# A state-space layer joined with linear attention: kernel products for two channels at a time, their halves summed in the next step

## The chip, the cores and the metric

The program runs on one core of one Trainium2 chip. A core has a matrix engine (TensorE, "PE" in the profile; "PEld" is its loading of weights, which runs beside it), three engines that work on vectors (VectorE "DVE", ScalarE "ACT", GpSimd "POOL"), a sync engine ("SP") that issues most of the transfers, and 16 DMA engines that carry them out. Tiles lie in an on-chip memory of 128 partitions; results of TensorE land in a separate small memory, PSUM, and another engine has to copy them out ("evict" them) before TensorE can use them again. Each engine works through its own list of instructions strictly in order, and waits at an instruction until what it needs is there.

The metric is the device time of one execution, in microseconds (us).

## The reference, cut to what matters

The input `A_u` has 2048 time steps of 512 channels. Two layers read it, and a gate mixes them.

```python
# layer A: a state-space model, as a long convolution
logdA = dt * (A_re + 1j * A_im)                    # 512 channels x 128 states
P = exp(logdA[:, :, None] * l[None, None, :])      # l = 0..2047
K = einsum("dn,dnl,dn->dl", Cc, P, dt * Bc).real   # one filter of 2048 taps per channel
y = irfft(rfft(u padded) * rfft(K padded))[:2048] + u * Dskip
# layer B: attention without a softmax over time, 32 heads of 16
phi = concat(softmax(+p), softmax(-p)); o = (phi_q @ kv) / (phi_q @ z + 1e-6); b = o @ wo
g = sigmoid((x * gate_w).sum(-1)); out = g * a + (1 - g) * b
```

What the change touches is `K`: a sum over 128 states for each of 512 channels and 2048 lags.

## The kernel before, in words

**Stages.** The first part (to about 100 us of the trace) loads the inputs, builds sine and exponential tables, transposes the input, computes the keys of layer B and the spectrum of the input. The second part, the convolution stage, goes through the 512 channels in 16 units of 32 channels, together with the queries of layer B.

**One unit.** A lag is split into a coarse and a fine part: lag = 64 x (0..31) + (0..63), so that the filter is a product of two small tables, summed over the 128 states. VectorE builds the coarse table `A` in two multiplications (`half`, called by A1 and A2, line 1053), which differ in which product of the complex factors they take; these are the "halves". It builds the fine table `R` in two more (lines 1071 and 1075, from an exponential `E` by ScalarE, its shifted twin `El` by VectorE, line 1013, and sines and cosines `cs` by ScalarE). `A` has 128 columns a channel: 2 halves x 2 parts (paired with the two parts of `R`) x 32 coarse lags. TensorE then multiplies `A` by `R` (`kgen_chunk`, lines 168 to 177, the rows "kps"): 32 weight columns at a time, four channels side by side in the array's four column strips. Here the constant `FOURS` (line 95) decides how the halves are summed:

- In 13 of the 16 units each channel takes four products, which PSUM adds up: 128 products a unit.
- In units 0, 7 and 15 VectorE adds the halves of the table first (`a3`, line 1064), and each channel takes two products: 64 products a unit.

Either way a unit leaves 512 numbers in each partition of PSUM. Two units share one PSUM tile and one eviction to `KD` (`kd`, line 1090); unit 14 is evicted alone, and unit 15 alone in two pieces.

Then comes the first half of a Fourier transform of the filters (`fft_stage_a`, lines 180 to 183, the rows "psA"): `KD` for four channels is the weights (64 columns are the fine lags), and a table `W1` of 128 columns (32 frequencies x 4 channels) is the moving operand; 16 products a unit, evicted to `XA`. Further on: second half of the transform ("psB", line 189, evicted to `XK`), multiplication with the input's spectrum ("t", line 1185), the way back ("psz", evicted to `Zr`, written to memory as `Zd`, line 1230, and read back transposed as `ZT`, line 1239), the last sum ("psy", line 1295), the gate (lines 1317 to 1323) and the output (line 1334).

**Groups.** Units 0 to 11 are taken in groups of four (128 channels), units 12 and 13 together (64 channels), unit 14 alone (32 channels), and unit 15 alone, by a path without the trip through memory (lines 1251 and 1308).

**What sets the order.** Nothing is scheduled at run time. The program is a list of nodes, each for one engine; a string (`ORDER`) is the order in which all nodes are issued, `SIDES` says for each eviction that could go to ScalarE or VectorE which of them takes it, and `RINGS` which PSUM ring a tile comes from. Each engine's list follows `ORDER`. Buffers come in rings of fixed size: one `KD`, one `A`, two `R`, one `ZT` (it shares its buffer, "ax", with layer B's rows `ax`), and so on; and there are eight lanes for transfers under way. Tables of ScalarE (sine, or exponential and logarithm) are swapped by an instruction (line 65) wherever the order goes from one kind to the other.

Of the kernel before, what the change touches and what calls it, by code (L numbers as in the profile page):

```python
# [43 lines left out]
def build_index_cols(nc, pool):  # L44
    idx_i = pool.tile([128, 1], I32, name="idx_i")
    nc.gpsimd.iota(idx_i[:], pattern=[[0, 1]], base=0, channel_multiplier=1)
    want = (("p", 0, 127), ("p31", 0, 31), ("p63", 0, 63), ("h16", 4, 7), ("h2", 4, 1), ("s5", 5, 3), ("b5", 5, 1), ("b6", 6, 1), ("h8", 0, 7), ("h4", 0, 3))
    t = pool.tile([128, len(want)], I32, name="ii")
    f = pool.tile([128, len(want)], F32, name="if")
    for k, (name, shift, mask) in enumerate(want):  # L50
        if shift:
            nc.vector.tensor_scalar(out=t[:, k:k + 1], in0=idx_i[:], scalar1=shift, scalar2=mask,
                                    op0=ALU.arith_shift_right, op1=ALU.bitwise_and)
        else:
            nc.vector.tensor_single_scalar(out=t[:, k:k + 1], in_=idx_i[:], scalar=mask, op=ALU.bitwise_and)
    return t, f, {name: f[:, k:k + 1] for k, (name, _, _) in enumerate(want)}
# [14 lines left out]
class Plan:  # L71

    DIGITS = "0123456789abcdefghijklmnopqrstuvwxyzABCDEFGHIJKLMNOPQRSTUVWXYZ-_"
    ORDER = ("0J0K0f0g0h0L0O0N0R0S2x0c0d0e0i0j0k1c1e0M1b000102030405090a0b1I1x0u0v0w0Y1d1o1z0U1f0x0y0z0V0P0W1A0607081p1B1q1J1K1Y0l0m0n"
             "0-0Z180_0X112P1g1-2y2N1Z2Q2B130r0s0t0A0B0C1_2A2O2C1y1C0o0p0q10190D0E0F2J2K2R1h1F1D0Q1G16122L2M2T2S2F142H2U2G171S2I2D2E2V"
             "2X2W152Y4v4w1N1O1r1s1t1i1j1k4u4B4C1E4J2v2w0G0H0I1H4F4K4D4N1Q0T1a2Z4E2-2_1U1V1P301W4G4x4O1M1l1m1n4L4M591X27314H1u1v1w4R4I"
             "28214P32335a1T344V4S3520224Q2324361L4T4U55374W4X4Z56254Y393a384-51574_521R58263b3d4y3c503e535h2z2a3f5d545i293g5l3h5b2b5e"
             "3J3i5c2d5f5g5t3j5j3k5k5m2e3l3m3n3K3o3p5u5n5o5v3L5w2f3M2c2g3q3v3r5p5x3w2o2h5q3x2i3y3C3z3A3B5r5y3E3D3s3t3u3N3P3F3Q3G3H3I3O"
             "2q3R3S2k3T2j3V3X3Y3U3W3Z3-2l3_5s402m412p4342442r2s4546472n484a4f2t494h2u4b4g4m4o4i704c4d4e4p727r4n7t5z7q7s4j4k4l4q4r4s5A"
             "5B5C5D5E4t5I6_5F5G5H714z734A7674777968696a6b7c5J78757d7a7i7e7D7j6c7b7f5K7g7E7h9a6d6e7F7J9c6f5L7R7S7T7k6g7l7u6h6z7v7K7x7w"  # L80
             "7A7m5M5N7n8O6i6j6k7-7_806A5O7y7z8X6B7B8P7o8Y5P7p7C6l6m6n6p6q6r6o6C7G7H7I8K7U7V7W6t5Q8M6u8L8Q7L8U5R8V8N6s5S5T5U5V8ZaD8R6D"
             "5W5X5Y7MaE916E6F927N7P7O7Q6G5-5_606H9d8S6v9e9m9n5Z8T9f61818W6I828-8_996w62836x6J6K6L6M6N6O9ba-90639j6Pb06y93946Q6R6S6465"
             "896T8h9k8a8i6U6V8485669o6W8b9s9g678c9h7X7Y7Z6XaA8daC9t6Y6Z6-9i8p8qazaB9l9D9E9Fa_9597b18j969p9q8r988kaFaM9raJ8687889u8l8s"
             "8e8f8gaGaN9vaKcw9w9y8m8n8o8t9xbb9zcyaHaIcxaLbcb2aOaSaTb3czaPb49MaQb89N8D9A9B9C9Ocob9aRaUbhcs9UaV9Vbd8u8v8w8x8y8zb58A8B8C"
             "9P9Q8E9G9H9I8F9R9S9T9Wb6cAcBcCa0a1djdk8G8H9J9K9La2bsbtbub7cDa8a9cEcF8I9XcGcHcIaWba9Y8Jbie8a3aaaXe9dsaba4bvbwbxbedl9Z9-9_"
             "bfdpaYdqdtaZbgacbjcpcJcKcLcNcOcPbkcMblbncQadaeafdmamctdybodncqbmbBbCbJbKa5a6a7dobRbpbqbrbDdrcubEbSduagahaid7d8d9bFbLbMdz"
             "bZbNbybzbAanb-dvdwdxcrbTcvdAdBbUb_bGbHbIc0eaaobObPbQajakaldCbVeeefc1dEbWbXbYapdFdDdGebecaqc2c3c4ardOdHdPasdadbdceddIegeB"
             "eCeEeFdQdJdgdhdicbeDeheHeic5c6c7eGeIejdKcccddRcRekdSdddedfeJeKc8c9cacedLdMdNeLeMeNeOcfelemencScgcTdTdUdVchePeQeoawaxayeR"
             "cUeSatauaveTepdWdXdYcVcWdZd-d_cZcXcYclcmcneUeVc-e0eWeqeresc_d0cicjcke1d1d2d3eXeYeteuevewexeyeZe5e6e7e2e3e4e-e_d4d5d6ezeA"
             "f3f4f5f0f1f2")  # L90
    SIDES = ("101001110101011000000100111001111100000011000100010000111101010000000100001100000000010000000000000000000000100000000001"
             "00010111111100000001100101000000010")
    RINGS = ("001011011111010000001010010001001010010010100100100100000110001100010101011110011011000000000000000000001110000000000001"
             "01011110001100000000010111010011100111001011001010010100111100000111110")
    FOURS = ("0111111101111110")
# [96 lines left out]
def prepare(P, nc, g, evict, psum):  # L192
# [297 lines left out]
    xt = []  # L490
# [42 lines left out]
def keys_and_spectrum(P, nc, g, psum):  # L533
# [85 lines left out]
    def shift():  # L619
        g.UD = g.wT = None  # L620
        g.shift()
# [398 lines left out]
def plan_conv(P, nc, g, psum, r):  # L1020
# [19 lines left out]
    def kgen(units, XA, new, split=False):  # L1040
        K = Bag()
        K.done, kps, nu = [], [], len(units)
        for cc, U in enumerate(units):
# [37 lines left out]
            def kp(c=c, cc=cc, four=four):  # L1081
                if cc == 0:
                    K.ps = psum([128, 2, 4, 2, 64], "kps")
# [489 lines left out]
```

## Time and profile before

| | |
|---|---|
| Median of 3 runs | 271.82 us (270.63 to 276.2) |
| The profiled execution's own time | 270.31 us |
| Its span, first to last instruction | 268.5 us |
| Mean granted clock of TensorE | 0.923 |
| Busy share: PE, DVE, ACT, POOL | 75%, 83%, 82%, 3% |
| Instructions | 10262 |

The profile is of one execution. A group of rows gives the line, the engine, the operation, what it writes and reads, the count, the busy time and the mean of one instruction in nanoseconds (ns). The mean counts an instruction from its start to its end; where instructions overlap at the edges, the distance from one start to the next is smaller, and this distance (its "pitch") is what the instruction costs an engine that has no idle time. Lines of the timeline give start, duration, engine, line, operation and count, and in brackets how long the engine had been idle before and what ended that. Reported idle time of an engine that nobody waits for costs nothing.

### The profile page before, as it was taken

Reading aid. Unit: us, or ns where it says so; the run is one execution under the profiler, and the core shown is the slowest. Engines: PE = TensorE matmul, PEld = TensorE weight load, DVE = VectorE, ACT = ScalarE, POOL = GpSimd, SP = SyncE. Lnnn points to the kernel's source line nnn. Section 1 sums busy time; section 2 is a strip of 40 time slices with the busy share of each in tenths; the row PEclk is TensorE's granted clock in tenths of the full one; section 3 lists DMA queues with packets and bytes.
Section 4 is the critical chain, followed back from the end, with each engine's and each line's share of the span. In section 5 each row is a group of like instructions: output and inputs, shape, how many; then the busy total and the mean of one; then the engine's idle time right before and its main releaser. Section 6 shows DMA issues by size and latency. Waiting matters only on the chain. (4 is left out here: it accounts for less than half of the span.)

```text
span 268.5 us, 10262 instructions
## 1 busy us (share of the span) xinstructions
PE 202.2 (75%) x4640; PEld 140.5 (52%) x4640; DVE 224.2 (83%) x300; ACT 219.1 (82%) x265; POOL 7.6 (3%) x16
## 2 busy tenths in 40 slices
PE   1358999999886679758587877876978779789810
PEld 1247666566655434435466755464747547665600
DVE  6999768698999789999999989995999889976401
ACT  6899799989899899999999989996788897644100
POOL 7300000000000000000000000000000000000000
PEclk9999999999999959999569999996897999999955
DMA  5999510000439894048055441392686899998372
GB/s 116 145 179 224 143 42 2 1 2 2 120 95 257 243 277 160 5 115 213 6 166 147 105 156 35 128 173 68 196 258 188 168 219 246 201 235 151 60 110 44
DMA packets 71468, 36.27 MB, mean 135 GB/s; under 512 B 50304, under 2 KB 66304, under 8 KB 71424
## 3 DMA queue, kind: packets, MB, share of 16 engines
q1 hardware_dynamic: 67680, 34.83, 56.0%
q10 hardware_dynamic: 3744, 0.79, 1.6%
q8 instruction: 36, 0.59, 0.9%
q14 instruction: 8, 0.07, 0.1%
HBM read 21.12 MB, written 13.11 MB: 127 GB/s over the span
## 5 line engine op out<-in xcount | busy, mean ns | idle before, releaser
L1053 DVE TENSOR_TENSOR A<-Ctab,Dtab 128x2048 bf16<-128x2048 bf16 x32 | 38.3, 1221 | 0.2
L68 ACT ACTIVATE cs<-args 128x1024 bf16<-128x1024 f32 x32 | 30.9, 1037 | 1.9 <-issue 1.1
L65 ACT ACT_TABLE_LOAD x18 | 23.1, 1283 | 0.3
L176 PE MATMUL kps<-R,A 128*32 128x64 bf16 x1856 | 20.3, 202 | 3.3 <-issue 2.1
L176 PEld LDWEIGHTS <-A 128*32 128x32 bf16 x1856 | 18.3, 116 | 6.6 <-issue 5.3
L1071 DVE TENSOR_TENSOR R<-E,cs 128x2048 bf16<-128x2048 bf16 x16 | 19.5, 1220 | 0.6 <-ACT E L68 0.6
L140 ACT CAST XK<-psB 128x1024 bf16<-128x1024 f32 (+1 forms) x15 | 14.3, 980 | 6.5 <-PE psB L189 6.3
L1075 DVE TENSOR_TENSOR R<-El,cs 128x2048 bf16<-128x2048 bf16 x16 | 19.5, 1220 | 0.1
L1185 DVE TENSOR_TENSOR t<-XUX,XK 128x2048 bf16<-128x2048 bf16 x14 | 17.1, 1220 | 2.1 <-ACT XK L140 1.3
L1217 PE MATMUL psz<-t,TI 128*128 128x512 bf16 x60 | 16.1, 395 | 2.8 <-ACT cs L68 2.6
L806 PE MATMUL pq<-xT,Wqp 128*128 128x512 bf16 x64 | 15.8, 393 | 2.6 <-ACT KD L140 2.2
L140 ACT CAST Zr<-psz 128x1024 bf16<-128x1024 f32 x15 | 15.3, 1032 | 2.7 <-PE psz L1217 1.2
L140 ACT CAST XA<-psA 128x1024 bf16<-128x1024 f32 (+1 forms) x15 | 13.9, 972 | 3.9 <-PE psA L183 3.8
L189 PE MATMUL psB<-XA,TB 128*128 128x128 bf16 (+2 forms) x192 | 11.2, 207 | 7.3 <-issue 3.3
L68 ACT ACTIVATE Ek<-pk 128x1024 bf16<-128x1024 f32 x16 | 15.4, 1024 | 1.4 <-PE pk L679 1.3
L68 ACT ACTIVATE E<-args 128x1024 bf16<-128x1024 f32 x16 | 16.4, 1042 | 0.2 <-PE args L1004 0.2
L68 ACT ACTIVATE Eq<-pq 128x1024 bf16<-128x1024 f32 x16 | 15.5, 1061 | 0.6 <-PE pq L806 0.6
L1320 DVE TENSOR_TENSOR xT<-psy,gT 128x1024 bf16<-128x1024 f32 (+1 forms) x5 | 5.6, 1116 | 11.8 <-PE psy L1295 11.8
L710 PE MATMUL vp<-WW,xT 128*128 128x512 bf16 x64 | 15.0, 379 | 0.0
L679 PE MATMUL pk<-WW,xT 128*128 128x512 bf16 x64 | 15.0, 379 | 0.0
L189 PEld LDWEIGHTS <-TB 128*128 128x128 bf16 x192 | 9.4, 100 | 9.7 <-issue 9.2
L497 PE MATMUL xps<-ident,UD 128*128 128x128 bf16 x64 | 7.3, 293 | 7.6 <-DMA UD<-in_A_u_dram 5.6
(203 smaller groups left out, 488.6 us busy)
## 6 DMA issues: line engine op xcount, KB each, us to landing
XUX<-XUd SPq DMA_DIRECT2D x32, 256.0 KB, 4.3
XUd<-xst SPq DMA_DIRECT2D x8, 512.0 KB, 4.4
ax<-apd SPq DMA_DIRECT2D x16, 256.0 KB, 5.2
Zd<-Zr SPq DMA_DIRECT2D x15, 256.0 KB, 3.6
ZT<-Zd SPq DMA_DIRECT2D x6, 512.0 KB, 7.2
UD<-in_A_u_dram SPq DMA_DIRECT2D x16, 128.0 KB, 4.3
XUd<-xst SPq DMA_DIRECT2D x8, 256.0 KB, 5.4
out_dram<-xT SPq DMA_DIRECT2D x4, 192.0 KB, 4.2
```

Of the source, the lines that this page charges most:

```text
L65: return self.nc.scalar.preload_act_table_set(name)
L68: return self.nc.scalar.activation(**kw)
L140: self.nc.scalar.copy(out=o, in_=i)
L176: nc.tensor.matmul(kps[32 * dj:32 * dj + 32, g4, e, :], lhsT=A[:, d // 4, 32 * ka:32 * ka + 32, d % 4], rhs=R[:, kr, d, :], start=(i == 0) ...
L189: nc.tensor.matmul(ps[:, sl, :], lhsT=fc.TB[:, 3 * (r0 + sl) + 1:3 * (r0 + sl) + 3].rearrange("p a b -> p (a b)"), rhs=XA[:, r0 + sl], sta ...
L679: nc.tensor.matmul(box.ps[:, u, :], lhsT=xT[:, 2 * s2 + u, kt, :], rhs=g.WW[:, kt, :], start=(kt == 0), stop=(kt == 3))
L806: nc.tensor.matmul(box.ps[:, m - m0, :], lhsT=g.Wqp[:, kt, 128 * m:128 * m + 128], rhs=xT[:, 4 * b:4 * b + 4, kt, :], start=(kt == 0), sto ...
L1053: nc.vector.tensor_tensor(out=c.A[:, :, 64 * k:64 * k + 64, :].rearrange("p q (x b) l -> p x b q l", b=8), in0=cf.unsqueeze(2).to_broadcas ...
L1071: nc.vector.tensor_tensor(out=c.R[:, :, :, 32:64], in0=t.E[:].unsqueeze(1).to_broadcast([128, 2, 32, 32]), in1=t.cs[:], op=ALU.mult)
L1075: nc.vector.tensor_tensor(out=c.R[:, :, :, 0:32], in0=t.L[:].unsqueeze(1).to_broadcast([128, 2, 32, 32]), in1=t.cs[:, ::-1, :, ::-1], op=A ...
L1185: nc.vector.tensor_tensor(out=box.t, in0=Ls[r0 // ns].X[:], in1=box.XK[:].unsqueeze(1).to_broadcast([128, 2, 1024]), op=ALU.mult)
L1217: nc.tensor.matmul(box.ps[:, hb, :], lhsT=fc.TI[:, k].rearrange("p t h a -> p (t h a)"), rhs=box.t[:, k, 512 * hb:512 * hb + 512], start=( ...
```

## The change

- Every unit now takes the same way: for each channel two products of 64 weight columns (32 coarse lags x 2 halves), summed in PSUM over the two parts of `R`; 64 products a unit. The halves stay apart, as neighbouring columns of `A`, and so as neighbouring rows of the result. Two channels lie side by side in the array instead of four. VectorE's additions `a3` are gone.
- A unit therefore leaves 1024 numbers in each partition of PSUM instead of 512. Each unit has a PSUM tile and an eviction to `KD` of its own.
- The first half of the Fourier transform takes two channels at a time instead of four. Its table `W2` has 64 columns (32 frequencies x 2 channels) and gives both halves of a coarse lag the same entry, so that the sum over the rows adds the halves up. It takes 32 products a unit, of 64 moving columns each, instead of 16 of 128.
- `W2` lies in the place of `W1` and is made from a small table (a sine and a cosine row more) by two VectorE instructions, once the input's spectrum has used `W1`.
- The index columns move to another tile, with one column more.
- `ORDER`, `SIDES` and `RINGS` are new throughout. Among other things some evictions change engine; unit 14's way through memory now comes ahead of that of units 12 and 13; the last outputs are all issued by ScalarE's queue.

```diff
-def kgen_chunk(nc, kps, A, R, four):
-    for e in range(2):
-        for g4 in range(4):
-            terms = [(k, k) for k in range(2)] if not four else [(0, 0), (2, 0), (1, 1), (3, 1)]
-            for i, (ka, kr) in enumerate(terms):
-                for dj in range(4):
-                    d = 8 * g4 + 4 * e + dj
-                    nc.tensor.matmul(kps[32 * dj:32 * dj + 32, g4, e, :], lhsT=A[:, d // 4, 32 * ka:32 * ka + 32, d % 4],
-                                     rhs=R[:, kr, d, :], start=(i == 0), stop=(i == len(terms) - 1), tile_position=(0, 32 * dj), skip_group_check=True)
+def kgen_chunk(nc, kps, A, R):
+    for i in range(16):
+        for o in range(2):
+            for dj in range(2):
+                d = 2 * i + dj
+                nc.tensor.matmul(kps[64 * dj:64 * dj + 64, i, :], lhsT=A[:, d // 4, 64 * o:64 * o + 64, d % 4], rhs=R[:, o, d, :],
+                                 start=(o == 0), stop=(o == 1), tile_position=(0, 64 * dj), skip_group_check=True)
...
 def fft_stage_a(nc, fc, ps, lhsT):
     for ri in range(2):
-        nc.tensor.matmul(ps[64 * ri:64 * ri + 64], lhsT=lhsT, rhs=fc.W1[:, ri].rearrange("p r d -> p (r d)"), start=True, stop=True, tile_position=(0, 64 * ri))
+        nc.tensor.matmul(ps[64 * ri:64 * ri + 64], lhsT=lhsT, rhs=fc.W2[:, ri].rearrange("p r d -> p (r d)"), start=True, stop=True, tile_position=(0, 64 * ri))
...
+    for i in range(2):
+        v, kv = turns(lambda: F.sm[:, 0:32], "sm", lambda: g.icol["q31"], one(12 + i), 32, 4 + i, "tg2")
+        sine(lambda i=i: g.w2[:, i, :], v, kv, f"w2{i}", nm="tgw")
...
+    def w2():
+        w, o = g.w2[:].rearrange("p i r -> p (i r)").unsqueeze(2), fc.W2.rearrange("p i r d -> p (i r) d")
+        nc.vector.tensor_scalar(out=o[:, :, 1:2], in0=w, scalar1=g.icol["b6"], scalar2=None, op0=ALU.mult)
+        nc.vector.tensor_tensor(out=o[:, :, 0:1], in0=w, in1=o[:, :, 1:2], op=ALU.subtract)
+    P.add("DVE", "w2", w2, rw=("w20 w21", "W1"))
...
-                nc.vector.tensor_tensor(out=c.A[:, :, 64 * k:64 * k + 64, :].rearrange("p q (x b) l -> p x b q l", b=8),
+                nc.vector.tensor_tensor(out=c.A[:].rearrange("p q (x b k) l -> p k x b q l", b=8, k=2)[:, k],
...
-            def a3(c=c):
-                nc.vector.tensor_tensor(out=c.A[:, :, 0:64], in0=c.A[:, :, 0:64], in1=c.A[:, :, 64:128], op=ALU.add)
...
-                if cc == 0:
-                    K.ps = psum([128, 2, 4, 2, 64], "kps")
-                kgen_chunk(nc, K.ps[:, cc], c.A, c.R, four)
+                box.ps = psum([128, 16, 64], "kps")
+                kgen_chunk(nc, box.ps, c.A, c.R)
...
-        d = evict2("KD", kd, [[], []], kps[0]) if split else [evict("KD", kd, kps[:1] + kps[1:])]
+            ds.append(evict2("KD", kd, [[], []], kps[0]) if split else [evict("KD", kd, kps)])
...
-                box.ps = psum([128, 8, 128], "psA")
-                for i in range(8):
-                    fft_stage_a(nc, fc, box.ps[:, i, :], K.KD[:, cc, i // 2, 64 * (i % 2):64 * (i % 2) + 64])
+                box.ps = psum([128, 16, 64], "psA")
+                for i in range(16):
+                    fft_stage_a(nc, fc, box.ps[:, i, :], K.KD[cc][:, i, :])
```

More of the change, by code (lines that the diff above doesn't have):

```diff
@@ L73 @@
     DIGITS = "0123456789abcdefghijklmnopqrstuvwxyzABCDEFGHIJKLMNOPQRSTUVWXYZ-_"
[L74 to L90, printed above, removed]
@@ L252, in low, with turns @@
         return v.bitcast(I16)[:, ::2]
-    def turns(src, ks, mul, add, n, small=None):
+    def turns(src, ks, mul, add, n, small=None, nm="tg1"):
         i = nv[0] % 3
@@ L261, in v, with sine @@
             return F.v[i][:, 0:n] if small is None else F.smv[:, small, 0:n]
-        V("tg1", lambda: nc.vector.tensor_scalar(out=v(), in0=src(), scalar1=mul(), scalar2=add(), op0=ALU.mult, op1=ALU.add), r="ic one " + ks, w=kv)
+        V(nm, lambda: nc.vector.tensor_scalar(out=v(), in0=src(), scalar1=mul(), scalar2=add(), op0=ALU.mult, op1=ALU.add), r="ic one " + ks, w=kv)
         return v, kv
-    def sine(out, v, kv, w, turn=False):
-        S("tgs", lambda: act(out=out(), in_=(low(v()) if not turn else low(v()).rearrange("p (h t) -> p t h", h=2)), func=ACT.Sin, scale=TURN), r=kv, w=w, tab="T")
+    def sine(out, v, kv, w, turn=False, nm="tgs"):
+        S(nm, lambda: act(out=out(), in_=(low(v()) if not turn else low(v()).rearrange("p (h t) -> p t h", h=2)), func=ACT.Sin, scale=TURN), r=kv, w=w, tab="T")
     one = lambda i: (lambda: F.one[:, i:i + 1])
@@ L650, in gc @@
         nc.vector.reciprocal(out=g.gT[:], in_=G.z[:])
-    a = P.add("PE", "gps", ga, xt, take=[("ps", "b2")], rw=("wsm", ""))
+    a = P.add("PE", "gps", ga, xt + [sp], take=[("ps", "b2")], rw=("wsm", ""))
     b = P.add("DVE", "g_b", gb, [a], drop=["psum"])
@@ L1041, in kgen @@
         K = Bag()
-        K.done, kps, nu = [], [], len(units)
+        K.done, K.KD, kps, ds, nu = [], {}, [], [], len(units)
         for cc, U in enumerate(units):
@@ L1045, in kgen @@
             plan_exp(P, nc, g, psum, U, t, psq, [sh])
-            four = P.FOURS[U] == "1"
             c = Bag()
```

89 lines of the change are left out of this document (55 added, 34 removed).

## The prediction

> **What bounds the kernel now.** I read the page's first lines, then the busy time by stage, then the chain that ended last, then single rows.
>
> ```profile
> span 268.5 us, 10262 instructions
> ```
> ```profile
> core 0: us, PE busy (x) PEld busy (x) DVE busy (x) ACT busy (x) POOL busy (x), PEclk, DMA share, GB/s
> 0.00:97.00 97.00, 74.37 (x1024) 51.80 (x1024) 82.56 (x145) 87.51 (x113) 7.59 (x16) 0.99 0.54 118
> 107.00:183.00 76.00, 55.96 (x1694) 39.60 (x1687) 73.12 (x78) 74.09 (x86) 0.00 (x0) 0.93 0.46 116
> 183.00:240.00 57.00, 47.82 (x1376) 35.95 (x1377) 49.36 (x51) 42.55 (x48) 0.00 (x0) 0.91 0.81 197
> 235.00:250.00 15.00, 13.19 (x315) 9.53 (x317) 10.04 (x16) 5.68 (x9) 0.00 (x0) 1.00 0.86 174
> 240.00:268.50 28.50, 14.38 (x494) 9.55 (x492) 10.04 (x16) 5.53 (x9) 0.00 (x0) 0.76 0.58 98
> ```
> ```profile
> by line: DMA ZT<-Zd 4.7%; issue 3.3%; PE psy L787 2.4%; PE psz L1217 2.4%; PE psB L189 2.1%; PE kps L176 1.8%; DMA XUX<-XUd 1.8%; PE psA L183 1.7%; PE psy L1295 1.7%; ACT XA L140 1.7%; DVE t L1185 1.3%; PE bps L905 1.3%; DVE xT L1320 1.1%;
> ```
>
> The reader should see four stages. Up to 97 us ScalarE is busy 87.5 us of 97. From 107 to 183 ScalarE and VectorE are both full (74.1 and 73.1 us of 76), and TensorE is not (56.0). From 183 to 240 VectorE (49.4 of 57) and TensorE (47.8) lead, and ScalarE has 14.5 us to spare. Behind 240 no engine is half busy but TensorE; that end is latency, and the chain names what it is made of: the reading of `ZT` back from memory, 4.7% of 268.5 us or 12.6 us. The change takes work from VectorE (additions), leaves TensorE's about equal, and adds evictions. So it matters who carries the evictions, and in which stage.
>
> **The change part by part.** The counts are from the two programs' instruction lists.
>
> ```profile
> L65 ACT ACT_TABLE_LOAD x18 | 23.1, 1283 | 0.3
> ...
> L140 ACT CAST KD<-kps 128x1024 bf16<-128x1024 f32 x6 | 6.1, 1022 | 0.0
> ...
> L1064 DVE TENSOR_TENSOR A<-A 128x2048 bf16<-128x2048 bf16 x3 | 3.7, 1221 | 0.0
> ...
> L142 DVE CAST KD<-kps 128x1024 bf16<-128x1024 f32 x1 | 1.2, 1224 | 0.7 <-PE kps L176 0.7
> ```
> ```profile
> 168.67 1.01 ACT L140 CAST KD<-kps 128x1024 bf16<-128x1024 f32 x1
> 169.56 1.03 ACT L140 CAST Zr<-psz 128x1024 bf16<-128x1024 f32 x1
> ```
> ```profile
> 232.80 1.22 DVE L1064 TENSOR_TENSOR A<-A 128x2048 bf16<-128x2048 bf16 x1
> 233.94 1.22 DVE L1075 TENSOR_TENSOR R<-El,cs 128x2048 bf16<-128x2048 bf16 x1
> ```
>
> *Pitches.* On a full engine a piece costs the distance to the next start: 169.56 - 168.67 = 0.89 us for an eviction of 1024 on ScalarE, 233.94 - 232.80 = 1.14 us for a table product on VectorE. For an eviction of 1024 on VectorE I take 1.14 too (1224 ns against 1221).
>
> *Additions of tables.* Three go: 3 x 1.14 = 3.4 us less on VectorE. Two of them stand in full stretches; the third is the row at 232.80, directly ahead of the last unit's last product of `R`.
>
> *Evictions to KD.* Before: seven of 1024, one of 512, two of 256, in all 8192 numbers a partition. After: fifteen of 1024 and two of 512, 16384. ScalarE's share goes from six to thirteen of 1024, VectorE's from one to two. That is eight whole evictions more: 7 x 0.89 = 6.2 us on ScalarE, 1.1 on VectorE. The halves of a table that VectorE added once in three units are now carried through PSUM in sixteen. The Trainium skill, "TensorEngine Tiling (Array Packing)", Performance Considerations, under PSUM Bottleneck, says that packing speeds up TensorE but not the emptying of PSUM, which can become the bottleneck. The rows of 107 to 183, where both engines that can empty PSUM are full, bear it out; what it would make of the time is the second rival.
>
> *Other pieces that change engine.* Up to the last product of unit 15's tables VectorE also gains two evictions of layer B's values, one of `XK`, one of `oT`, one half-sized of `Y`, the table `selE` (from GpSimd) and a dozen tiny pieces, and loses the two of the folded weights, one `t` and one product with the gate, which move behind that point. With pieces of 1024 or 2048 at 1.14 and half-sized ones at half of that this is +4.6 +0.6 +0.6 +0.6, -2.3 -1.1 -0.6: +2.4. With the additions (-3.4) and its one `KD` (+1.1), VectorE's list up to that point is +0.1 us. Of this, +1.1 lies before the convolution stage. ScalarE up to the last `E` (unit 15's): six `KD` +5.3, two folded weights +1.8, two `XK` -1.8, two values -1.8, two `Y` of half size -0.9, one table load fewer (18 in place of 19) -1.3, small pieces +0.4: +1.7. Behind that point it gets the rest. So the new lists have moved work so that the two engines end about as far apart as before. ScalarE is 1.7 later already at its eighth `cs`, where the stage that it leads ends (two folded weights, a table load that comes sooner and small pieces, less two values).
>
> *TensorE.* No row shows products of 64 weight columns of `A`. The nearest are those of 64 columns that layer B has, with 68 moving columns, and the old transform's, with 128.
>
> ```profile
> 50.56 0.71 PE L728 MATMUL kvp<-vr,Ek 128*64 128x68 bf16 x32
> 51.20 0.63 PE L562 MATMUL psA<-W,UDp 128*128 128x256 bf16 x4
> ```
> ```profile
> 123.23 0.64 PE L183 MATMUL psA<-W,KD 128*64 128x128 bf16 x16
> 123.80 1.26 PE L176 MATMUL kps<-R,A 128*32 128x64 bf16 x128
> 125.26 0.39 PE L982 MATMUL args<-selE,statC 64*128 64x512 bf16 x2 [0.19 <-DVE XA L142]
> ```
>
> (51.20 - 50.56)/32 = 20 ns a product; the old transform (123.80 - 123.23)/16 = 36 ns; an old four-term unit 125.26 - 0.19 - 123.80 = 1.27 us for 128, 9.9 ns each. The new unit's 64 products cost 64 x 20 = 1.28 us, were they like layer B's; 64 x 9.9 = 0.63 us were the width free; 64 x 36 = 2.3 us were they like the transform's. I take 20, the row with the same weights and nearly the same moving columns: equal to before in 13 units, and about 0.65 more in the three whose 64 narrow products took half of 1.27. The new transform, 32 products of 64 by 64, at 20 is 0.64 us against 0.57. Altogether 3 x 0.65 + 16 x 0.07 = +3 us of TensorE over 140 us; between -10 (0.63 a unit) and +16. From 107 to 183 TensorE has 20 us free and hides the +3. The new order needs no PSUM tile that waits for a second unit, which I count as nothing.
>
> *Start and W2.* Two more sines (ScalarE) and some ten pieces of one column to 64 on VectorE; they are in the sums above. `W2` is written over `W1` after the spectrum's last use and long before the first new transform: nothing waits.
>
> *The end.* Here the order itself changes.
>
> ```profile
> 176.15 0.38 PE L787 MATMUL psy<-wo 128*128 128x128 bf16 x4 [0.31 <-ACT E L68]
> ...
> 178.48 0.39 PE L982 MATMUL args<-selE,statC 64*128 64x512 bf16 x2
> ```
> ```profile
> 243.57 1.02 PE L1217 MATMUL psz<-t,TI 128*128 128x512 bf16 x4
> 244.44 1.03 PE L905 MATMUL bps<-wo,oT 128*128 128x512 bf16 x4
> ...
> 251.63 0.65 PE L1295 MATMUL psy<-ZT,TJ 64*32 64x64 bf16 x60
> 252.75 0.21 PE L1295 MATMUL psy<-ZT,TJ 64*32 64x64 bf16 x4 [0.47 <-issue]
> ```
> ```profile
> 245.88 0.43 SPq L1230 DMA_DIRECT2D Zd<-Zr  x1
> 253.19 0.84 SPq L1334 DMA_DIRECT2D out_dram<-xT  x2
> 257.00 2.56 SPq L1239 DMA_DIRECT2D ZT<-Zd  x2
> 264.32 1.51 SPq L1334 DMA_DIRECT2D out_dram<-xT  x2
> ```
>
> Before, unit 14's `Zd` is issued at 245.88, but its `ZT` is read only at 257.00: the one buffer is held by units 12 and 13 until 252.96, and the sync engine takes 4 us more. From 257.00 to the end it is 11.5 us. After, unit 14 goes first, and units 12 and 13 wait for the buffer. Count from the last product of `R`, at 233.94 + 1.22 = 235.2 before. One more pitch (the second half of `A` comes behind it), and unit 15's products start at 236.3 on that scale. TensorE's list from there to the sum that frees the buffer holds what it did between 235 and 250 (13.2 us busy) with, beyond it, the eight steps of layer B for the third channel group and their `psy` (178.48 - 176.15 = 2.3, and about 0.6), a `psz` (0.9) and unit 14's last sum (0.8), without unit 14's `psB` (0.8): 17 us, so 253.3. If the sync engine issues the read then, the last 11.5 us follow, and 1.8 more: a gated product of 1024 in place of 512 and four outputs from one queue in place of two from each of two. That is 266.6: 1.9 us earlier than 268.5. It is 3.7 earlier if ScalarE's queue takes its outputs at no cost, and 2 later if the sync engine loses its 4 us again.
>
> **Sum.** Start +1.1 (VectorE) to +1.7 (ScalarE), I take +1.2, since either leads there; the convolution stage 0 (VectorE's list -1.0, ScalarE's tighter by 5); the end -1.9. Span 267.8. The profiled execution lasted 270.31 us, 1.8 more than its span, so 269.6. The median of the three runs, 271.82, is 1.5 above that execution; the range has to hold this too. About 2% is what a measurement of this kernel can tell from no change.
>
> **The rivals.**
>
> 1. *TensorE is fed more steadily* (faster). The page counts time in which TensorE waited for nothing shown:
>
> ```profile
> q8 instruction: 36, 0.59, 0.9%
> ```
>
> "Issue" is 3.3% of the chain, 8.9 us. A transfer of instructions is 0.59 MB / 36 = 16 KB. A four-term unit with its transform takes 128 + 16 products, now 64 + 32, a third fewer. If the waits come from instructions arriving late, and shrink by a half on the chain, that is -4.5: 265. With VectorE's -1.0 as well it is 264. Against it: all of TensorE's list shrinks only from 9282 to 8130 rows, an eighth.
>
> 2. *ScalarE becomes the bound* (slower). The place is 107 to 183, where it has 1.9 us left. The price is the eight evictions at 0.89, 7.1 us, with nothing taken off, because VectorE then waits for `KD`, `XA` and `XK` instead of leading; with the start and the end as above 269.6 + 7.1 = 276.7. It decides from the point where the added evictions there (five, for ten units, 4.5 us) exceed the 1.9 spare and the 14.5 us of later idle time can't be reached because `E` for the next unit stands behind them. Against it: the list up to the last `E` is only 1.7 longer.
>
> 3. *The wide products are no cheaper than the old transform's* (the change doesn't do what it says). At 36 ns a unit takes 2.3 us, 1.0 more; from 183 on, where TensorE has 9 us free and leads, six units add up to 6: 275.6.
>
> **How the numbers follow.** My forecast, VectorE sets the pace and only the end moves, gets 0.5 and covers 266 to 273 (the end between -3.7 and +2, the start, and the spread of the runs). Rival 1 gets 0.2 (262 to 266), rival 2 0.22 (273 to 280), rival 3 0.08. Leaving out the outer half of rivals 1 and 2, the range is 264 to 277. Faster than 264.9 (2%): most of rival 1, 0.19. Slower than 275.7: most of rival 2, half of rival 3 and a little of the forecast, 0.25. Within: 0.56.
>
> **What the new profile would show.** Thirteen `KD` rows on ScalarE near 0.89 pitch, no addition; 64 products of `A` in 1.2 to 1.3 us (0.6 or 2.3 would move the sum to the rivals); VectorE without idle up to the last `R`, which ends near 236; the read of units 12 and 13's `ZT` issued near 253 with its last `psy` near 260. Wrong would make it: ScalarE full and VectorE waiting for `XK` or `E` between 107 and 183 (rival 2), shorter "issue" stretches (rival 1), or an end that waits on a queue that I did not name.

## The result and the profile after

The changed kernel takes 278.31 us (median of 4 runs, 277.47 to 279.71), beside 271.23 us for the kernel before (4 runs): 1.028 times as long, with a 95% interval of 1.020 to 1.036. It is slower, and outside the predicted range. The ratio leaves out one run of the kernel before, of 276.2 us, that lay apart from the other three. The profiled execution of the changed kernel lasted 279.71 us, with a span of 277.8.

The page's first line, and the busy time by stage, read as in the prediction:

```profile
span 277.8 us, 9147 instructions
```
```profile
core 0: us, PE busy (x) PEld busy (x) DVE busy (x) ACT busy (x) POOL busy (x), PEclk, DMA share, GB/s
0.00:97.00 97.00, 71.94 (x1020) 50.81 (x1021) 81.37 (x148) 84.65 (x111) 6.12 (x15) 0.99 0.48 109
107.00:183.00 76.00, 63.05 (x1271) 46.24 (x1270) 68.47 (x79) 69.81 (x85) 0.00 (x0) 0.94 0.35 95
183.00:240.00 57.00, 46.79 (x992) 35.58 (x994) 51.35 (x51) 49.27 (x52) 0.00 (x0) 0.96 0.74 188
240.00:277.80 37.80, 24.26 (x752) 18.36 (x752) 14.85 (x20) 10.77 (x17) 0.00 (x0) 0.84 0.75 126
```

Between 107 and 183 TensorE does 7.1 us more than before (63.05 against 55.96), while VectorE and ScalarE do 4.7 and 4.3 less. So neither is the bound there: both now wait for something. The costliest groups of instructions (first fence) and the waits between 103 and 245 us (second) name it:

```profile
L1062 DVE TENSOR_TENSOR A<-Ctab,Dtab 128x2048 bf16<-128x2048 bf16 x32 | 38.7, 1219 | 4.7 <-PE kps L174 4.5
L174 PE MATMUL kps<-R,A 128*64 128x64 bf16 x1024 | 34.0, 228 | 3.3 <-ACT E L68 1.0 <-DVE R L1081 0.8 <-DVE A L1062 0.8
...
L140 ACT CAST KD<-kps 128x1024 bf16<-128x1024 f32 x13 | 13.3, 1023 | 5.8 <-PE kps L174 5.8
```
```profile
ACT KD L140 <- PE kps L174: 5.8, 6, 2.4
...
DVE A L1062 <- PE kps L174: 4.5, 3, 2.7
...
DVE t L1192 <- ACT XK L140: 4.3, 2, 3.8
```

In the kernel before, the two rows of `A` and of its products were these:

```profile
L1053 DVE TENSOR_TENSOR A<-Ctab,Dtab 128x2048 bf16<-128x2048 bf16 x32 | 38.3, 1221 | 0.2
...
L176 PE MATMUL kps<-R,A 128*32 128x64 bf16 x1856 | 20.3, 202 | 3.3 <-issue 2.1
```

The 1024 products of `A` take 34.0 us, 33 ns each and 2.1 us a unit, where the forecast had 20 ns and 1.28 us. Two queues stand behind them: VectorE's, whose next table `A` has one buffer, and ScalarE's, where `KD` stands ahead of other work.

The sync engine's DMA issues (start, duration) show the two other places. First the kernel before, then the changed one, then what the changed one's last read of `ZT` waits for:

```profile
28.85 3.63 SPq L351 DMA_DIRECT2D statE<-pz  x8
...
68.39 28.35 SPq L599 DMA_DIRECT2D XUd<-xst  x16
```
```profile
72.08 12.07 SPq L603 DMA_DIRECT2D XUd<-xst  x8
84.19 6.04 SPq L355 DMA_DIRECT2D statE<-pz  x8
90.34 8.79 SPq L603 DMA_DIRECT2D XUd<-xst  x8
...
258.42 2.21 SPq L1341 DMA_DIRECT2D out_dram<-xT  x4
264.61 1.96 SPq L1246 DMA_DIRECT2D ZT<-Zd  x2
```
```profile
SPq L1246 <- DMA out_dram<-xT: 3.9, 1, 3.9
```

The reads of `statE` now stand between the writes of `XUd`. The reads of `ZT` for units 12 and 13 stand behind four outputs, and are issued 4.5 us after the sum that freed their buffer; 3.9 us of this the sync engine waits for an output under way. These are the rows of that sum, of the second half of the last `psy`, and of its product with the gate; and, from the timeline of VectorE, the first product of `A` (before, then after) and the last of `R`:

```profile
99.71 2.36 DVE L1053 TENSOR_TENSOR A<-Ctab,Dtab 128x2048 bf16<-128x2048 bf16 x2
```
```profile
103.56 2.36 DVE L1062 TENSOR_TENSOR A<-Ctab,Dtab 128x2048 bf16<-128x2048 bf16 x2
...
239.95 1.22 DVE L1081 TENSOR_TENSOR R<-El,cs 128x2048 bf16<-128x2048 bf16 x1
...
259.47 0.66 PE L1302 MATMUL psy<-ZT,TJ 64*32 64x32 bf16 x64
...
270.56 0.61 PE L1302 MATMUL psy<-ZT,TJ 64*32 64x64 bf16 x32 [0.86 <-DMA ZT<-Zd]
...
271.22 1.23 DVE L1327 TENSOR_TENSOR xT<-psy,gT 128x1024 bf16<-128x1024 f32 x1 [5.67 <-PE psy L1302]
```

The first `A` and the end of the last `R` cut each span into three parts, which the rest of this text uses:

| us | before | forecast | after |
|---|---|---|---|
| start, to the first `A` | 99.7 | 100.9 | 103.6 |
| stage, to the end of the last `R` | 135.4 | 135.5 | 137.6 |
| end | 33.3 | 31.4 | 36.6 |
| span | 268.5 | 267.8 | 277.8 |

The 10.0 us by which the forecast of the span failed are 2.7 in the start, 2.1 in the stage and 5.2 in the end. These are single executions, and one list of instructions can differ from itself by more than the 2.1 us of the stage: the profiles below that keep the changed kernel's work in the stage, with products of 33 ns, have stages of 135.1 to 137.6 us.

### The profile page after: what moved, and what is told of

The parts are those of the page before. It is cut to its first block, busy times and chain, and to the rows that moved or that the text cites. A ratio compares the mean times of both kernels' runs of the same rounds, so it can differ in the third digit from the quotient of the medians.

```text
span 277.8 us, 9147 instructions
## 1 busy us (share of the span) xinstructions
PE 213.6 (77%) x4064; PEld 153.1 (55%) x4064; DVE 222.3 (80%) x305; ACT 224.4 (81%) x273; POOL 6.1 (2%) x15
## 4 chain that ended last, share of the span: by engine, by line
PE 36%; ACT 23%; DVE 14%; DMA 9%; SPq 9%; issue 7%; ACTq 0%; DVEq 0%
PE kps L174 7%; ACT cs L68 4%; DMA ax<-apd 4%; PE pq L816 4%; DVE A L1062 3%; ACT Ek L68 3%; PE vp L720 3%; PE psz L1224 3%; PE pk L689 2%; SPq L603 2%; DVE Eq L883 2%; PE psy L797 2%; SPq L355 2%; DMA wT<-in_B_wqkv_dram 2%; PE psA L181 2%
## 5 line engine op out<-in xcount | busy, mean ns | idle before, releaser
L1062 DVE TENSOR_TENSOR A<-Ctab,Dtab 128x2048 bf16<-128x2048 bf16 x32 | 38.7, 1219 | 4.7 <-PE kps L174 4.5
L174 PE MATMUL kps<-R,A 128*64 128x64 bf16 x1024 | 34.0, 228 | 3.3 <-ACT E L68 1.0
L174 PEld LDWEIGHTS <-A 128*64 128x64 bf16 x1024 | 32.8, 156 | 6.0 <-issue 2.7
L1077 DVE TENSOR_TENSOR R<-E,cs 128x2048 bf16<-128x2048 bf16 x16 | 19.5, 1217 | 0.8 <-PE kps L174 0.4
L140 ACT CAST KD<-kps 128x1024 bf16<-128x1024 f32 (+1 forms) x15 | 14.4, 965 | 6.9 <-PE kps L174 6.9
L1081 DVE TENSOR_TENSOR R<-El,cs 128x2048 bf16<-128x2048 bf16 x16 | 19.5, 1216 | 0.1
L140 ACT CAST Zr<-psz 128x1024 bf16<-128x1024 f32 x14 | 14.4, 1039 | 2.5 <-PE psz L1224 2.0
L181 PEld LDWEIGHTS <-KD 128*64 128x64 bf16 x512 | 9.9, 115 | 8.2 <-ACT KD L140 4.4
L181 PE MATMUL psA<-W,KD 128*64 128x64 bf16 x512 | 11.5, 200 | 3.6 <-ACT KD L140 2.7
L992 PE MATMUL args<-selE,statC 64*128 64x512 bf16 x32 | 7.1, 432 | 8.6 <-ACT cs L68 3.4
```

The costliest lines, as they stand in the source:

```text
L140: self.nc.scalar.copy(out=o, in_=i)
L174: nc.tensor.matmul(kps[64 * dj:64 * dj + 64, i, :], lhsT=A[:, d // 4, 64 * o:64 * o + 64, d % 4], rhs=R[:, o, d, :], start=(o == 0), stop= ...
L181: nc.tensor.matmul(ps[64 * ri:64 * ri + 64], lhsT=lhsT, rhs=fc.W2[:, ri].rearrange("p r d -> p (r d)"), start=True, stop=True, tile_positi ...
L1062: nc.vector.tensor_tensor(out=c.A[:].rearrange("p q (x b k) l -> p k x b q l", b=8, k=2)[:, k], in0=cf.unsqueeze(2).to_broadcast([128, 8, ...
L1077: nc.vector.tensor_tensor(out=c.R[:, :, :, 32:64], in0=t.E[:].unsqueeze(1).to_broadcast([128, 2, 32, 32]), in1=t.cs[:], op=ALU.mult)
L1081: nc.vector.tensor_tensor(out=c.R[:, :, :, 0:32], in0=t.L[:].unsqueeze(1).to_broadcast([128, 2, 32, 32]), in1=t.cs[:, ::-1, :, ::-1], op=A ...
```

## The experiments

Each ratio is to the kernel before in runs on the same chip, with its 95% interval. Expectations are quoted as they stood before the run.

### The products of TensorE

**Weights side by side.** In `kgen_chunk`:

```
-lhsT=A[:, d // 4, 64 * o:64 * o + 64, d % 4]
+lhsT=A[:].rearrange("p q x l -> p (q x l)")[:, 64 * (2 * d + o):64 * (2 * d + o) + 64]
```

> The changed kernel, but each of the 64 products of a unit takes its 64 weight columns from 64 neighbouring numbers of the table A, in place of every fourth number (other numbers are multiplied, so the output is not the reference's; all counts and sizes stay). Theory W (the step of four numbers between weight columns makes a product 32 ns): a unit's products fall from 2.05 us to 1.25 to 1.3, the waits of VectorE's A for these products (4.5 us) and of KD (7 us) shrink by half, and the time falls by 2 to 4 us, to 274 to 276. Rival D (a product waits for the sum that was written two products earlier into the same place): still 2.05 us, no change. Rival L (the products are off the path, the loss is the start and the end): 1.28 us, and the time falls by less than 1 us.

Ratio 1.004 (0.999 to 1.009), where the changed kernel has 1.028: 2.4%, or 6.5 us, less. The groups of this kernel:

```profile
L1062 DVE TENSOR_TENSOR A<-Ctab,Dtab 128x2048 bf16<-128x2048 bf16 x32 | 38.8, 1224 | 2.2 <-PE kps L174 2.1
...
L174 PE MATMUL kps<-R,A 128*64 128x64 bf16 x1024 | 20.7, 202 | 4.2 <-DVE A L1062 2.1 <-DVE R L1081 0.8 <-ACT E L68 0.5
...
L140 ACT CAST KD<-kps 128x1024 bf16<-128x1024 f32 x13 | 13.5, 1041 | 2.3 <-PE kps L174 2.3
```

The products now take 20.2 ns, the waits of `A` and `KD` half as long, and the stage is 129.1 us (first `A` at 104.53, last `R` ending at 233.62): 8.5 us less than in the changed kernel and 6.3 less than before. The gain is larger than any theory had it, and larger than the stage differs between executions. The step between weight columns is the cause of the 33 ns, and the kernel pays for it.

**A step of two.** `A` has innermost runs of two numbers in place of four; the products read it so, and `half` writes it with the same change:

```
-c.A = g.wk.tile([128, 8, 128, 4], BF16, ...)
+c.A = g.wk.tile([128, 16, 128, 2], BF16, ...)
-lhsT=A[:, d // 4, 64 * o:64 * o + 64, d % 4]
+lhsT=A[:, d // 2, 64 * o:64 * o + 64, d % 2]
```

> The changed kernel with the table A laid out so that weight columns are two numbers apart in place of four; everything is computed. Theory W: products between 20 and 32 ns, near 20 as layer B's, whose step is two; 1.28 us a unit, the time as with neighbouring numbers if VectorE writes the table at the same 1.14 us pitch. If VectorE pays for the shorter runs of two numbers, its 32 products of the table show it in their 1219 ns, and each 100 ns more costs 3.2 us over the kernel. Rival D: 2.05 us as before.

Ratio 1.063 (1.056 to 1.071), slower still:

```profile
L1062 DVE TENSOR_TENSOR A<-Ctab,Dtab 128x2048 bf16<-128x2048 bf16 x32 | 61.7, 1948 | 1.8 <-PE kps L174 1.8
...
L174 PE MATMUL kps<-R,A 128*64 128x64 bf16 x1024 | 23.1, 211 | 12.8 <-DVE A L1062 9.9 <-DVE R L1081 1.3 <-DVE gz L659 1.1
```

The products fall to 22.6 ns as theory W has it, but VectorE writes the table in 1948 ns in place of 1219, 23 us over the kernel. The layout is a bargain between two engines: VectorE's product is fast with runs of four and slow with runs of two (the edit shortens the runs that it reads as well as those that it writes), and TensorE's products are slow at a step of four.

**Sums further apart.** The loops take the channel pairs i and i + 8 in turn:

```
-    for i in range(16):
+    for i0 in range(8):
         for o in range(2):
-            for dj in range(2):
+            for i, dj in [(i0 + i1, dj) for i1 in (0, 8) for dj in range(2)]:
```

> The changed kernel with the products of two channels taken in turn, so that two products into the same place are four apart in place of two; everything is computed. Theory W: 2.05 us a unit and no change of the time (277 to 280). Rival D: near 1.28 us a unit, and the time falls by 2 to 4 us.

Ratio 1.030 (1.025 to 1.036), 33.9 us of products. The distance between sums into one place does nothing; rival D falls.

**Two narrow products for a wide one.**

```
+for h in range(2):
+    c0 = 64 * dj + 32 * h
+    nc.tensor.matmul(kps[c0:c0 + 32, i, :], lhsT=A[:, d // 4, 64 * o + 32 * h:64 * o + 32 * h + 32, d % 4], ..., tile_position=(0, c0))
```

> The changed kernel with each product of 64 weight columns written as two of 32 columns side by side, on their own strips of TensorE, into the same places of PSUM: 128 products a unit, and everything else as in the changed kernel; everything is computed. The weights keep their step of four numbers. Theory W2 (loads of four strips of 32 columns run beside each other, as the 9.9 ns a product of the kernel before show; the step costs only where 64 columns go in one load): 1.27 us a unit in place of 2.05, and the time falls as it did with neighbouring weights, by 4 to 7 us, to 271 to 274. Rival C (the cost goes by the number of strided columns, 0.5 ns each, however they are split): 128 products at 16 ns, 2.05 us, no change.

Four runs spread from 279.15 to 288.32 us, too far for a ratio, but none is near 274. The products did fall to 22.6 us for 2048, 11 ns each, so that theory W2 is right about their length and wrong about the time. The run was repeated with both late transfers (below) moved:

> The changed kernel with both moved steps and with each product of 64 columns written as two of 32 columns on strips of their own; everything is computed. The products take 11 ns each and 1.3 to 1.4 us a unit, as short as with neighbouring weights, but there are 1024 more of them. Theory I (TensorE stands still where its next instructions arrive late, and 1024 more products bring those waits back): waits on issue of 6 us or more between the first product of A and the last of R, and a time above that of the same kernel with 64 products a unit (273), 276 to 284. Rival (only the length of the products counts; the single run of this form was slow by disturbance): 266 to 269, as with neighbouring weights.

Ratio 1.036 (1.029 to 1.042); the same kernel with 64 wide products a unit has 1.009, and with wide products of 20 ns 0.980 (both below). So the number of products counts. Against the second of these kernels the products are nearly as short (22.7 us beside 20.5), yet the stage is 141.0 us in place of 127.8. TensorE's waits for nothing that the profile shows, between 100 and 242 us (us in total, times, longest):

```profile
PE kps L176 <- issue: 3.6, 4, 1.7
PE psy L799 <- issue: 3.2, 1, 3.2
PE zs L839 <- issue: 3.2, 2, 1.7
PE psA L183 <- issue: 1.2, 2, 0.9
```

That is 11.2 us; the kernel with wide products of 20 ns has 0.3 in its stage. The longest of them on the timeline, and the DMA queues in just that stretch, 201.17 to 204.34 (packets, MB, share of the 16 engines):

```profile
204.34 0.38 PE L799 MATMUL psy<-wo 128*128 128x128 bf16 x4 [3.17 <-issue]
```
```profile
q1 hardware_dynamic: 897, 0.80, 94.0%
q8 instruction: 1, 0.02, 2.9%
```

One transfer of instructions falls into the gap, beside data that keeps the 16 DMA engines busy to 94%. But full DMA engines are no condition. The next wait, of 1.7 us, stands where the DMA share is 0.00; from 108.8 us to its end a single transfer of instructions is all that moves.

```profile
111.60 0.30 PE L839 MATMUL zs<-Eq,KVbd 128*32 128x128 bf16 x8 [1.68 <-issue]
```

The longest gap of the kernel before looks the same, 180.27 to 183.55:

```profile
183.55 0.80 PE L189 MATMUL psB<-XA,TB 128*128 128x128 bf16 x6 [3.28 <-issue]
```
```profile
q1 hardware_dynamic: 801, 0.58, 81.8%
q8 instruction: 1, 0.02, 2.9%
```

What the waits share is the end of such a transfer: in the two traces, between 100 and 242 us, each of the nine waits on issue here and of the five in the kernel before ends 1.2 to 1.6 us after a transfer of instructions has ended. So it is the next instructions that TensorE waits for.

**The wide products in the old order.** The kernel before, with the loops of the changed kernel's `kgen_chunk`; the channel pairs i and i + 8 share a place:

```
+nc.tensor.matmul(kps[64 * dj:64 * dj + 64, i // 2 % 4, i % 2, :], lhsT=A[:, d // 4, 64 * o:64 * o + 64, d % 4],
+                 rhs=R[:, o, d, :], start=(o == 0), stop=(o == 1), tile_position=(0, 64 * dj), ...)
```

> The kernel before, in its own order, with the 64 products of 64 columns of the changed kernel in every unit, written into its 512 numbers of PSUM (two channels share a place, so the output is not the reference's). TensorE gets 0.78 us more in thirteen units and 1.4 in three, 14.4 us. Theory W (the products alone make the loss): 276 to 280, 5 to 8 us above the kernel before. Rival O (the new order makes the loss, the old one covers longer products in TensorE's 20 free us from 107 to 183): at most 2 us above.

Ratio 0.991 (0.984 to 0.998): a little faster. Theory W falls. Rival O holds, and neither had foreseen a gain. Its groups of the products and of `KD`, and its queue of instructions:

```profile
L174 PE MATMUL kps<-R,A 128*64 128x64 bf16 x1024 | 34.2, 228 | 0.9 <-ACT XK L140 0.3 <-ACT E L68 0.3 <-DVE A L1051 0.2
...
L140 ACT CAST KD<-kps 128x1024 bf16<-128x1024 f32 x6 | 6.1, 1017 | 0.0
```
```profile
q8 instruction: 29, 0.48, 0.8%
```

The products are as long as in the changed kernel, 14 us more than before, and the old order hides them. `A` waits 2.2 us for them in place of 4.5, and ScalarE's whole pieces of `KD`, six for two units each, not at all. And between 100 and 242 us TensorE has no wait on issue left, where the kernel before has these, 6.0 us:

```profile
PE psB L189 <- issue: 3.3, 1, 3.3
...
PE kps L176 <- issue: 2.1, 3, 1.4
...
PE psy L787 <- issue: 0.6, 1, 0.6
```

The kernel has 8578 instructions in place of 10262, and 29 transfers of them in place of 36.

**Half of the narrow products.** To see whether number or length makes that gain:

```
-terms = [(k, k) for k in range(2)] if not four else [(0, 0), (2, 0), (1, 1), (3, 1)]
+terms = [(k, k) for k in range(2)]
```

> The kernel before with the four-term units cut to two terms (half of the sum is left out, so the output is not the reference's): 1024 products of 32 columns in place of 1856, TensorE's list as short as with the 64-column products in the kernel before, and 0.63 us less of products a unit where those had 0.78 more. Theory I (what the kernel before gains from fewer products is TensorE's waits for its own instructions, 9.7 us before and none with 1024 wide products): the waits on issue go here as well, and the time is 267 to 270, as with the wide ones. Rival P (TensorE's time counts): 1.4 us less a unit than with the wide products shows, 262 to 266.

Ratio 0.994 (0.988 to 1.000), with 12.0 us of products in place of the 34.2 above, and again no wait on issue worth the name (0.2 us). With the same number and a third of the length the time is the same within the intervals. So in the old order their length does not count. That their number does is less sure by the time alone, with gains of 0.9% and 0.6% and intervals that reach 0.998 and 1.000; theory I rests as much on the waits, which are gone in both.

### ScalarE

Only the first half of each `KD` is evicted:

```
-hs = slice(0, 16) if k is None else slice(8 * k, 8 * k + 8)
+hs = slice(0, 8) if k is None else slice(4 * k, 4 * k + 4)
-fft_stage_a(nc, fc, box.ps[:, i, :], K.KD[cc][:, i, :])
+fft_stage_a(nc, fc, box.ps[:, i, :], K.KD[cc][:, i % 8, :])
```

> The changed kernel with only the first half of each unit's KD moved out of PSUM (512 numbers in place of 1024; the transform reads each of them twice, so that the output is not the reference's). The prediction's rival that ScalarE is the bound: thirteen pieces on ScalarE lose 0.4 us each, 5.3 us, and the time falls by 4 to 5 us. My reading of the two traces (ScalarE had 4.3 us less to do between 107 and 183 than before, and waited for the products): the time falls by at most 2 us, from KD's own delay between the products and the transform.

Ratio 1.022 (1.014 to 1.030), 0.6% or 1.7 us below the changed kernel and within the intervals. The group of `KD` shows that it waits a little longer in return:

```profile
L140 ACT CAST KD<-kps 128x512 bf16<-128x512 f32 x13 | 7.8, 596 | 6.3 <-PE kps L174 6.2
```

5.5 us were taken off ScalarE, and by the ratio 1.7 of them came out, where the rival had 4 to 5. Some gain is likely: the stage of this execution, 133.5 us, lies 1.6 below the lowest of those with whole evictions. But `KD` still waits for the products, so ScalarE is not the bound.

### The late transfers

**statE.** One node moves in `ORDER`; on the sync engine's list:

```
 statC<-pz x8
+statE<-pz x8
 XUd<-xst x8
-statE<-pz x8
 XUd<-xst x8
```

> The changed kernel with one step moved: the eight reads of statE are issued straight behind those of statC, near 30 us, in place of 84 us, between the writes of XUd; everything is computed. Theory Q (the sync engine's queue is the start's loss: the writes of XUd stand 6 us behind statE's reads, xst waits for them and the sines of cs behind it): the second half of the XUd writes is issued 4 to 6 us sooner, the first product of A starts at 100.5 to 101.5 in place of 103.6, and the time falls by 2 to 3 us. Rival V (the lists of ScalarE and VectorE up to there are longer, by the 1.2 us of the prediction and more): A starts no sooner than 103, the time stays within 1 us.

Ratio 1.022 (1.015 to 1.029). The first `A` starts at 101.28. The seven profiles of the changed kernel's order without this step have it between 103.6 and 105.2, the four with the step between 100.8 and 101.3. So the place in the queue is worth 2.3 us or more of the start. By the ratios it is 0.6% of the time, 1.7 us, which lies within the two intervals; the run of both steps, below, settles it.

**ZT.** Likewise, for units 12 and 13:

```
 Zd<-Zr
+ZT<-Zd x2
 out<-xT x4
-ZT<-Zd x2
```

> The changed kernel with one step moved: the two reads of ZT for units 12 and 13 are issued ahead of the four output transfers of the third channel group in place of behind them; everything is computed. Theory T (the read waits 3.9 us for the transfers ahead of it, with its buffer already free at 260.1): the read is issued 4 us sooner on the scale of the changed kernel's profile, within 0.7 us of the end of the psy that frees its buffer, and the time falls by 3.5 to 4.5 us, to 274 to 275. Rival E (the four outputs then end last, or the read takes longer beside them): less than 2 us.

Ratio 1.022 (1.015 to 1.029), 1.7 us less than the changed kernel. Rows of its timeline:

```profile
259.21 0.66 PE L1302 MATMUL psy<-ZT,TJ 64*32 64x32 bf16 x64
...
260.11 2.61 SPq L1246 DMA_DIRECT2D ZT<-Zd  x2
...
267.82 0.34 PE L1302 MATMUL psy<-ZT,TJ 64*32 64x64 bf16 x11 [1.22 <-issue]
```

The read is issued 0.2 us behind the sum that frees its buffer, where it was 4.5. Of these 4.3 us 1.2 go to a wait on issue in the last `psy`; the end is 34.0 us in place of 36.6. Theory T has the mechanism and over-states its price.

**Both steps.**

> The changed kernel with both moved steps, the early reads of statE and the early reads of ZT; everything is computed. If the two losses are separate places (start 2.3 us, end 2.8 us by the profiles of the two single runs), they add: 4 to 5 us below the changed kernel, 272.5 to 274.5, within 1% of the kernel before, and what is left is the convolution stage. Rival (the stage or the DMA queues take up what comes sooner): no lower than 276.

Ratio 1.009 (1.004 to 1.013): 2.0% below the changed kernel, 5.3 us, and clear of its interval. By the parts of the spans the two add (2.3 and 2.6 us); by the ratios they give more together than 1.7 and 1.7, within the intervals. What is left above the kernel before is about 1%.

**Both steps and neighbouring weights.**

> The same with the 64 weight columns of a product from neighbouring numbers (other numbers are multiplied, so the output is not the reference's): what the change would be with products of 20 ns, as the prediction took them, and without its two late transfers. If the three terms add (6.5, 2 and 2 us by the ratios): 266 to 269, 2 to 3% faster than the kernel before, the stage from the first product of A to the last of R 129 to 130 us in place of 137.6. Rival (they overlap): 270 or more.

Ratio 0.980 (0.971 to 0.988). The three terms add within their intervals. The stage is 127.8 us (100.86 to 228.68). Had the products been as short as forecast, and had the two transfers stood earlier, the change would have been 2% faster than the kernel before.

**The same step in the kernel before**, for unit 14's `ZT`:

```
 Zd<-Zr
-out<-xT x2
 ZT<-Zd x2
+out<-xT x2
```

> The kernel before with one step moved: the two reads of unit 14's ZT are issued ahead of the two output transfers that stood before them; everything is computed. Its read stood at 257.00 with its buffer free at 252.96. The read comes 3 to 4 us sooner, and the time falls by 2 to 3.5 us, to 0.987 to 0.993 of the kernel before. Rival (Zd of unit 14 or the crowded DMA engines hold it anyway): within 1 us of the kernel before.

Ratio 0.977 (0.968 to 0.985), 265.6 us median: the fastest kernel of this study that computes everything, faster than both. Its read of `ZT`:

```profile
248.18 0.65 PE L1295 MATMUL psy<-ZT,TJ 64*32 64x64 bf16 x60
249.31 0.21 PE L1295 MATMUL psy<-ZT,TJ 64*32 64x64 bf16 x4 [0.49 <-issue]
...
249.56 2.40 SPq L1239 DMA_DIRECT2D ZT<-Zd  x2
```

The read comes right behind the sum, and from the end of the last `R` (232.05) to the end of the span (260.9) it is 28.9 us in place of 33.3. The ratio says 2.3%, more than these 4.4 us; the rest lies in the stage of this execution, 132.7 us in place of 135.4, which the step does not touch. So much differs between executions of one list. What the step is worth is nearer to 4.4 us, 1.6%. Beside this kernel, which has the early read of `ZT` too, the change with all three places mended (0.980) shows no gain: the two intervals cover each other.

## Why the prediction was wrong

**TensorE's products.** This is the step that failed: "I take 20, the row with the same weights and nearly the same moving columns". That row, `kvp`, loads weights that are two numbers apart, `A`'s are four apart, and the runs give 20.2, 22.6 and 33 ns at steps of one, two and four. The rivals named 36 ns as possible, put it at 0.08, and priced it at 6 us; the measured price in this order is 6.5. In all the products took 14 us more than before, where the forecast had 2. (The prediction's bounds, -10 and +16, are distances from the 20 ns that it took; from the kernel before its own terms give about -7 and +19.5.) The step could be read in the code: the address step of the weights belongs to the operation as much as its size does.

**"TensorE has 20 us free and hides" it.** Between 107 and 183 TensorE is still idle for 13 us, and the products are not hidden. Free time of an engine hides a longer operation only if nobody stands behind it in an ordered queue. In the old order `KD` of two units is evicted at once and later, and the same products cost nothing; in the new one `KD` and the next `A` stand right behind each unit's products. That this place in the order makes the difference is read from the waits and not shown by a run, since the two orders differ throughout. How the cost splits between the two waits was not settled either: no run gives `A` a second buffer.

**The stage at 0.** Two errors of opposite sign met here, and that the stage came out only 2.2 us longer than before is luck. With 20 ns it is 129.1 and 127.8 us in two executions, against 135.4 and, in the early-`ZT` run of the old list, 132.7, where the forecast had no change. Two things went that can account for it: the additions (3.4 us of VectorE), and TensorE's waits on issue between the first `A` and the last `R`, 5.4 us before and none in the changed kernel. How the gain splits between them was not measured. So rival 1 was right about its mechanism; its size (4.5 us) was not measured in this order, and in the old one the waits went with a gain of 1.5 to 2.5 us. I argued it away by the eighth by which the whole list shrinks; the waits do not shrink in proportion, they vanish. The Trainium skill, "Runtime: NRT & Kernel Launch", Instruction fetch mechanics, says that an engine's instructions are fetched ahead in blocks of 16 KiB and that the cost of a block's end is mostly hidden. In the stage it is all but hidden in the runs with 29 to 32 blocks, and not in those with 36 or 39, where single blocks stop TensorE for up to 3.3 us.

**The start.** The forecast counted ScalarE's and VectorE's lists, +1.2; it came out at +1.1 to 1.6 in the kernels that have `statE` early (100.8 to 101.3 against 99.7). It missed a step that the new order moves: eight reads, 6.0 us of the sync engine, from 28.85 us, beside those of `statC`, to between the writes of `XUd`. (The traces show 17 table loads of ScalarE in place of 18, not 18 in place of 19; the difference of one, which the sum uses, stands.) The prediction followed the issues of the end, and not those of the start.

**The end.** The forecast chose the read of `ZT` straight behind its buffer, and named as its bound "2 later if the sync engine loses its 4 us again". It did lose them, to the same cause as before, outputs issued ahead. That is 2.6 us by the single run. The unit's products are 0.8 us longer. The rest, about 1.8 us, is spread over a list that waits for evictions; what in it is whose was not settled. From the read to the end it is 13.2 us, as forecast (11.5 + 1.8).

**ScalarE as the bound** (0.22) falls: it had work taken off and did not pass it on. Its time of 276.7 lay near the measured one by luck. The rule on emptying PSUM that stood beside that rival (the Trainium skill, "TensorEngine Tiling (Array Packing)", Performance Considerations) speaks of a TensorE that got faster, and did not decide here: TensorE's work grew, between 107 and 183 the two engines that empty PSUM do less than before, and half of `KD` taken away moved the time by 0.6%.

**The signs that were named.** Thirteen `KD` rows on ScalarE, no addition, and the new transform at 0.63 us for 32 products came as forecast. The products (2.1 us), VectorE's idle time, the last `R` (241.2 in place of 236), the read of `ZT` (264.6 in place of 253) and the last `psy` (270.6 in place of 260) did not, and the prediction had named them as what would speak for rival 3 and for a queue that it had missed.

## What to carry to other kernels

Price an operation by a row with the same address steps, not only the same shape; and before calling a longer operation hidden, look up who stands behind it in an ordered queue. When a list is reordered, follow every queue's list from end to end: here two late transfers cost 5.3 us together, nearly as much as the longer products, and one of the two steps, taken in the old kernel, gave the fastest version. So give the old kernel the same repair before crediting it to a change. Fewer, longer instructions can pay a little (0.9% here) although their engine gets busier, where that engine sometimes waits for its instructions.

## What the hardware did that was not expected

- The address step of 64 weight columns, on half of TensorE's columns, sets what a short product costs: 20.2 ns with neighbouring numbers, 22.6 ns with a step of two (4 bytes), 33 ns with a step of four (8 bytes). Products of 32 columns at the same step of four, on four strips in turn, run at 11 ns. The Trainium skill, "SBUF — State Buffer", Door 1: The DMA port swizzle (its note on cachelines), says that steps of up to eight bf16 numbers are free; for these weights the runs show that four are not.
- VectorE makes a table product of 2048 numbers in 1219 ns with runs of four numbers, and in 1948 ns with runs of two.
- TensorE's instructions come in transfers of 16 KB that share the DMA engines with data. With 36 and 39 of them in the span TensorE stood still for up to 3.3 us at a time, with 29 to 32 hardly at all in the stage. A wait ended 1.2 to 1.6 us after a transfer had ended, also where no data moved beside it.
